# One attention-and-FFN decode kernel: its first group moved into the loop, TensorE's program walked in two outer trips, and w_down dealt unevenly over the partitions

## The chip, the cores and the metric

The kernel runs on one core of a Trainium2 chip. The metric is the device time of one execution in microseconds. The kernel before takes 292.81 us, the median of three runs (292.75 to 292.83).

## The reference

One decode step of a transformer block for two sequences (B = 2, one query each, D = 640): layer norm, attention of 32 heads of width 192 over the last 2048 positions of a cache, a residual, layer norm again, a gated FFN (F = 1536), a residual. All in bf16.

```python
q = (layernorm(x) @ wq)                       # [2, 32 heads, 192]
k = k_cache[:, :, 8192 - 2048:, :]            # [2, 32, 2048, 192]
v = v_cache[:, :, 8192 - 2048:, :]
p = softmax((q . k) * 192 ** -0.5)
h = x + (p . v).reshape(2, 1, 6144) @ wo
n = layernorm(h)
out = h + (gelu(n @ w_gate) * (n @ w_up)) @ w_down
```

Nearly all bytes are read once: 50 MB of keys, 50 MB of values, 7.9 MB each of wq and wo, and 5.9 MB of FFN weights.

## The kernel before, in words

**Groups.** The 2 x 32 heads are cut into 16 groups g of four heads of one sequence. A group's keys are one load of 24,576 bytes on each of 128 partitions, its values another. `transposes(g, half)` turns the keys on TensorE (48 transposes of 128 x 128 f32 words, each a pair of bf16) into two PSUM pairs, and VectorE (L588) and ScalarE (L584) copy them to SBUF. `scores(g)` multiplies them with the masked q (`rq`, made on POOL by `q_masked`), `softmax(g)` finds the maximum (L651, L653) and exponentiates (L655), `e_columns(g)` turns the probabilities (L664), `pv(g)` multiplies by the values (L680). After every fourth group `z_rows`, `o_rows`, `o_columns` and `oproj` make one quarter J of the heads' output and its product with wo.

**Order of the work.** It is written out by hand. `_Prog` records every operation with what it reads and writes, works out which semaphore value each must wait for, and prints each engine's program. TensorE's and VectorE's groups 1 to 15 stand in a loop of four trips (`emit_loop`), in segments named a0 to d2; four groups make a trip. In a loop a wait's value is linear in the trip: S x trip + a. Segments that only some trips need stand under an `If`: "oc" and "op" (o_columns and oproj of the quarter before), and d0 to d2, which the last trip leaves out. Group 0, with q's product (`q_rows`, L598: 80 matmuls; `q_stationary`, L616: 12), stands ahead of the loop, and group 15's rest and the FFN behind it.

**Loads.** All large loads are issued by SP in one order into a ring of six slots in SBUF (`load`, `pump`, L363): K0, wq, K1, V0, K2, V1 and so on, wo's quarters between them, then w_gate, w_up (two pieces) and w_down (four pieces). A load is issued when the pieces that lay in its place have been read. ScalarE issues x and the first fifth of w_gate.

**FFN.** `ffn_in` multiplies the normalized h with w_gate, later with w_up: for each of five chunks of 128 rows, four matmuls of 384 columns on four groups of 32 rows of the array. The 1536 results lie in four row groups r; `ffn_columns` (L831) turns them with three f32 transposes of 98 rows into columns of 128 partitions, twelve columns per sequence. VectorE and ScalarE make gelu of gate and the product with up (`uT`). w_down has 12 rows on each partition, in four pieces of 6, 3, 2 and 1 rows (`WDC`); each row takes four matmuls of 160 columns into `m1` (L871: 48 in all). VectorE copies the result (L877), and SP stores it (L878).

Of the kernel before, what the change touches and what calls it, by code (L numbers as in the profile page):

```python
# [27 lines left out]
LOOPED = ("pe", "dve")  # L28
RARE = ("oc", "op")

# [24 lines left out]
class _Prog:  # L55
# [63 lines left out]
    def resolve(self, strides):  # L119
# [110 lines left out]
TPG = 64  # L230
WDC = ((0, 6), (6, 9), (9, 11), (11, 12))
WUC = ((0, 4), (4, 5))
# [3 lines left out]
WQ_AT = 3 * SLOT + SLOT // 2  # L236
WO_AT = (K_AT[3], K_AT[3], K_AT[2], 0)
WD_AT = (K_AT[2] + 15360, 15360, 19200, 19200 + 2560)


def bass_sequential_preLN__sliding_block_cached__geglu_ffn__decode_kernel(
# [12 lines left out]
    with ExitStack() as ctx:  # L254
# [75 lines left out]
        urow = osb  # L330
        gsb = sb("gsb", [128, NF * B], F32)
        ga = sb("ga", [128, 4, NF * B], F32)
        uT = sb("uT", [128, NF, 18], BF16)

# [7 lines left out]
        P = _Prog()  # L342


# [51 lines left out]
        def load_ffn():  # L396
            load(("wg", 1), K_AT[1], 2 * (NC5 - 1) * F, B_w_gate.rearrange("(p c) f -> p c f", c=NC5)[:, 1:NC5, :],
                 lambda v: v.rearrange("p (c f) -> p c f", f=F), "wg1")
            for i, (c0, c1) in enumerate(WUC):
                load(("wu", i), K_AT[3] + 2 * c0 * F, 2 * (c1 - c0) * F, B_w_up.rearrange("(p c) f -> p c f", c=NC5)[:, c0:c1, :],  # L400
                     lambda v: v.rearrange("p (c f) -> p c f", f=F), f"wu{i}")
            wd = B_w_down.rearrange("(q p s) n -> q p s n", p=128, s=6)
            for i, (f0, f1) in enumerate(WDC):
                q = f0 // 6
                load(("wd", i), WD_AT[i], 2 * (f1 - f0) * D, wd[q][:, f0 - 6 * q:f1 - 6 * q, :],
                     lambda v: v.rearrange("p (s n) -> p s n", n=D), f"wd{i}")


        def dve(fn, R=(), W=(), X=(), cls=1):
            return P.op("dve", fn, R, W, X, cls=cls)  # L410

        def act(fn, R=(), W=(), X=()):
            return P.op("act", fn, R, W, X)

# [40 lines left out]

        dve(lambda e: e.memset(eps_t[:, :], EPS), W=["eps"])
        dve(lambda e: e.memset(onesd[:, :], 1.0 / D), W=["onesd"])
# [39 lines left out]

        pe(_x_T, R=["xrow", "identb"], X=["m2"])
        dve(lambda e: e.tensor_copy(xT[:, :, :].rearrange("p c b -> p (c b)"), m2[:, 0:10]), W=["xT"], X=["m2"])
# [91 lines left out]
        def q_rows():  # L591
            wq, wtoks = where["wq"]

            def fn(e):
                for c in range(NC5):
                    for J in range(4):
                        for r in range(4):
                            ins = e.matmul(tps[0][32 * r:32 * (r + 1), 0:384], lhsT=xnT[:, c, 32 * J:32 * (J + 1)],  # L598
                                           rhs=wq[:, c, 1536 * J + 384 * r:1536 * J + 384 * (r + 1)],
                                           start=(c == 0 and J == 0), stop=(c == NC5 - 1 and J == 3), tile_position=(0, 32 * r))  # L600
                return ins

            pe(fn, R=["xnT"] + wtoks, X=[("t", 0)], cls=1)
            done("wq")
            act(lambda e: e.activation(
                out=qrow[:, :, :, :],
                in_=tps[0][:, 0:384].rearrange("p (h d) -> p h d", h=2).unsqueeze(2).to_broadcast([128, 2, 2, DH]),
                func=ACT.Copy, scale=SCALE), W=["qrow"], X=[("t", 0)])

# [49 lines left out]
        def e_columns(g):  # L659

            def fn(e):
                for u in range(4):
                    o = m2[:, 0:256].rearrange("p (ch u x) -> p ch u x", ch=4, u=4)[:, :, u, :]
                    ins = e.matmul(o, lhsT=eexp[:, 128 * u:128 * (u + 1)], rhs=sel64[:, :], start=True, stop=True)  # L664
                return ins

            pe(fn, R=["eexp", "sel64"], X=["m2"])
            o = 8 * (g % 4)
            dve(tt(ering[:, g % 4, :, o:o + 8].rearrange("p (a h) x -> p a h x", h=2),
                   m2[:, 0:256].rearrange("p (a h x) -> p a h x", h=2, x=8),  # L670
                   mask16[:, :].rearrange("p (h x) -> p h x", h=2).unsqueeze(1).to_broadcast([128, 16, 2, 8]), ALU.mult),
                R=["mask16"], W=[("er", g % 4)], X=["m2"], cls=0)

# [80 lines left out]

        transposes(0, 0)
        transposes(0, 1)
        q_rows()
        q_stationary()
        consts_late()
        scores(0)  # L760
        softmax(0)
        for J in range(4):
            for p in range(1, 5 if J < 3 else 4):
                g = 4 * J + p
                seg = "abcd"[p - 1]
# [14 lines left out]
                pv(g - 1)  # L780
                scores(g)
                if p == 4:
                    o_rows(J)
                softmax(g)
# [28 lines left out]
        def ffn_in(bank, xt, key, parts, loads):  # L813
            for c0, c1 in parts:
# [3 lines left out]
                def fn(e, c0=c0, c1=c1, wv=wv, l0=loads[i][0]):  # L818
                    for c in range(c0, c1):
                        for r in range(4):  # L820
                            cols = wv[:, c - l0, 768 * (r // 2):768 * (r // 2 + 1)].rearrange("p (x s) -> p x s", s=6)
                            ins = e.matmul(bank[32 * r:32 * r + 2, 0:384], lhsT=hnT[:, c, :], rhs=cols[:, :, 3 * (r % 2):3 * (r % 2) + 3],
                                           start=(c == 0), stop=(c == NC5 - 1), tile_position=(0, 32 * r))
                    return ins
# [3 lines left out]
        def ffn_columns(row, tok, bank, i):  # L828
            def fn(e):
                for j in range(3):  # L830
                    ins = e.transpose(bank[:, 128 * j:128 * j + 98], row[0:98, j:384:3], identf[0:98, 0:98])  # L831
                return ins

            pe(fn, R=[*tok, "identf"], X=[("t", i)])
            return bank[:, 0:384].rearrange("p (j r y) -> p r j y", j=3, y=32)[:, :, :, 0:2]

# [5 lines left out]

        def rjb(t):
            return t.rearrange("p (r j b) -> p r j b", r=4, j=3)

# [4 lines left out]
        pe(h_rows, R=["hrow", ("hsel", 0), ("hsel", 1)], X=["m1"])  # L850
        gT = ffn_columns(grow, ["sm"], tps[0], 0)
        dve(lambda e: e.tensor_copy(rjb(gsb[:, :]), gT), W=["gsb"], X=[("t", 0)])
        dve(tt(ga[:, 0, :], gsb[:, :], gsb[:, :], ALU.mult), R=["gsb"], W=["ga0"])
# [9 lines left out]
        vT = ffn_columns(urow, [("osb", 0), ("osb", 1)], tps[1], 1)  # L863
        dve(tt(uT[:, :, 0:17:16].rearrange("p (r j) b -> p r j b", r=4), vT, rjb(ga[:, 0, :]), ALU.mult), R=["ga0"], W=["uT"], X=[("t", 1)])
        for i, (f0, f1) in enumerate(WDC):
            wd, wtoks = where["wd", i]

            def fn(e, f0=f0, f1=f1, wd=wd):
                for f in range(f0, f1):
                    for r in range(4):  # L870
                        ins = e.matmul(m1[32 * r:32 * r + 17, 0:160], lhsT=uT[:, f, 0:17],  # L871
                                       rhs=wd[:, f - f0, 160 * r:160 * (r + 1)], start=False, stop=(f == NF - 1),
                                       tile_position=(0, 32 * r), skip_group_check=True)
# [7 lines left out]

        P.resolve({("dve", 0): 4 * 9, ("dve", 1): 8, ("act", 0): 4 * 3, ("pool", 0): 4})
        sems = {}
        for e, c in (("pe", 0), ("pe", 1), ("act", 0), ("dve", 0), ("dve", 1), ("pool", 0)):
            sems[e, c] = ctx.enter_context(nc.semaphore(f"s_{e}{c}"))
# [37 lines left out]
```

## Time and profile before

| What | Value |
|---|---|
| median of three runs | 292.81 us |
| the profiled execution | 292.58 us |
| its span, first to last instruction | 291.3 us |
| TensorE matmul / weight load busy | 198.6 us (68%) / 147.6 us (51%) |
| VectorE / ScalarE / POOL busy | 122.8 us (42%) / 76.9 us (26%) / 25.7 us (9%) |
| bytes read, mean rate over the span | 122.29 MB, 420 GB/s |
| instructions | 5093 |
| granted TensorE clock, mean | 0.871 of full |

Busy times of engines add up to more than the span, since the engines run beside each other. A wait on an engine that is not the last costs nothing. The DMA rows of the page are the mean over the core's 16 DMA engines. "q1" is the queue of the kernel's large transfers, "q10" that of ScalarE's, "q8" and "q14" those over which programs' code is loaded. A transfer raises its semaphore step by step as the DMA engines that share it finish, and the trace records each step; a waiting instruction goes on at the last.

### The profile page before, as it was taken

How to read it: one execution, taken by the hardware profiler on the slowest of the kernel's cores; microseconds unless marked ns; L12 is line 12 of the kernel's file. 1: busy time of each engine (PE TensorE's matmuls, PEld its weight loads, DVE VectorE, ACT ScalarE, POOL GpSimd, SP SyncE). 2: the span in 40 equal slices, each digit the busy share in tenths (PEclk: the TensorE clock that was granted, in tenths of full speed). 3: DMA queues.
4: the chain of work that ended last, by engine and by line, in shares of the span. 5: the costliest groups of instructions: out<-in, count | busy, mean ns of one | idle time of the engine just before them, and what ended most of it. 6: DMA issues, size and time to landing. Idle time of an engine off the chain costs nothing.

```text
span 291.3 us, 5093 instructions
## 1 busy us (share of the span) xinstructions
PE 198.6 (68%) x2141; PEld 147.6 (51%) x2141; DVE 122.8 (42%) x231; ACT 76.9 (26%) x72; POOL 25.7 (9%) x85
## 2 busy tenths in 40 slices
PE   0650868786668288768677478868478778496684
PEld 0640437566355175637374475645465746472341
DVE  4350025455435334635356244635247445253331
ACT  1050014333322122423222123523142333151001
POOL 8820073000000000000000000000000000000000
PEclk9997568999979869997989579999689799688957
DMA  8999999999999999999999999999999999999994
GB/s 324 432 440 422 428 432 432 428 429 429 428 419 440 432 432 432 429 432 432 432 416 448 432 432 430 432 412 429 432 432 425 422 432 432 429 432 434 420 411 181
DMA packets 6506, 122.44 MB, mean 420 GB/s; under 512 B 734, under 2 KB 864, under 8 KB 1504
## 3 DMA queue, kind: packets, MB, share of 16 engines
q1 hardware_dynamic: 6348, 121.90, 97.8%
q10 hardware_dynamic: 148, 0.40, 0.4%
q8 instruction: 7, 0.11, 0.2%
q14 instruction: 3, 0.02, 0.0%
HBM read 122.29 MB, written 0.00 MB: 420 GB/s over the span
## 4 chain that ended last, share of the span: by engine, by line
DMA 73%; PE 18%; DVE 3%; issue 2%; SPq 2%; ACT 1%; DVEq 0%
DMA ring<-in_A_k_cache_dram 54%; PE tpp L574 13%; DMA ring<-in_A_wq_dram 10%; DMA ring<-in_B_w_down_dram 9%; DVE ktr L588 3%; PE tpp L598 2%; SPq L363 2%; PE ops L680 1%; DVE ering L428 1%; ACT ktr L584 1%; PE m L731 1%; PE m L713 1%; PE m L871 0%; PE m L694 0%; DVE yrow L877 0%
## 5 line engine op out<-in xcount | busy, mean ns | idle before, releaser
L574 PE MATMUL tpp<-identf,ring 128*128 128x128 f32 x768 | 116.2, 314 | 39.3 <-DMA ring<-in_A_k_cache_dram 25.2
L574 PEld LDWEIGHTS tpp<-identf,ring 128*128 128x128 f32 x768 | 102.8, 163 | 47.5 <-DMA ring<-in_A_k_cache_dram 26.5
L588 DVE COPY ktr<-tpp 128x2048 bf16<-128x2048 bf16 x64 | 78.4, 1224 | 91.4 <-PE tpp L574 91.4
L584 ACT ACTIVATE ktr<-tpp 128x2048 bf16<-128x2048 bf16 x32 | 60.1, 1877 | 94.9 <-PE tpp L574 94.9
L655 ACT ACTIVATE eexp<-sm,nm 128x512 bf16<-128x512 f32 x16 | 11.6, 722 | 71.7 <-DVE nm L653 71.7
L635 PE MATMUL sps<-ktr,rq 128*16 128x512 bf16 x384 | 25.7, 402 | 1.1 <-POOL rq L428 1.1
L680 PE MATMUL ops<-ring,ering 128*32 128x384 bf16 x512 | 25.0, 339 | 0.0
L644 DVE CUSTOM_DVE_ANT_1 sm<-sps,mska 128x512 f32<-128x512 f32 x16 | 11.0, 686 | 27.0 <-issue 27.0
L428 POOL TENSOR_TENSOR rq<-qs,mask 128x96 bf16<-128x96 bf16 x16 | 5.5, 354 | 175.6 <-PE sps L635 154.1
L680 PEld LDWEIGHTS ops<-ring,ering 128*32 128x32 bf16 x512 | 12.7, 99 | 8.5 <-issue 2.8
L635 PEld LDWEIGHTS sps<-ktr,rq 128*16 128x16 bf16 x384 | 8.9, 89 | 14.4 <-issue 5.5
L651 PEld LDWEIGHTS m<-mrhs,pm 128*128 128x128 bf16 x16 | 1.5, 96 | 22.9 <-DVE mrhs L424 22.9
L651 PE MATMUL m<-mrhs,pm 128*128 128x16 bf16 x16 | 2.9, 184 | 14.8 <-DVE mrhs L424 14.8
L598 PE MATMUL tpp<-ring,xnT 128*32 128x384 bf16 x80 | 6.1, 499 | 9.4 <-DMA ring<-in_A_wq_dram 9.4
L598 PEld LDWEIGHTS tpp<-ring,xnT 128*32 128x32 bf16 x80 | 3.4, 143 | 11.9 <-issue 9.6
L621 DVE CAST qs<-ops 128x384 bf16<-128x384 f32 x1 | 0.6, 558 | 15.8 <-PE ops L616 15.8
L428 DVE TENSOR_TENSOR ering<-m,mask 128x256 bf16<-128x256 f32 x16 | 6.6, 415 | 1.3 <-PE m L664 1.3
L713 PE MATMUL m<-selb,orow 128*128 128x2 bf16 x48 | 3.5, 200 | 5.2 <-DVE ering L428 4.5
L713 PEld LDWEIGHTS m<-selb,orow 128*128 128x128 bf16 x48 | 3.2, 159 | 6.0 <-DVE ering L428 4.9
L664 PE MATMUL m<-sel,eexp 128*128 128x64 bf16 x64 | 4.8, 200 | 1.2 <-ACT eexp L655 1.2
L494 PE MATMUL m<-identb,xrow 2*128 2x2 bf16 x5 | 0.3, 173 | 7.4 <-DMA xrow<-in_A_x_dram 7.4
L428 DVE TENSOR_TENSOR orow<-m,wm 128x1536 bf16<-128x1536 f32 x3 | 5.3, 1751 | 0.0
(127 smaller groups left out, 93.6 us busy)
## 6 DMA issues: line engine op xcount, KB each, us to landing
ring<-in_A_k_cache_dram SPq DMA_DIRECT2D x16, 3072.0 KB, 29.5
ring<-in_A_v_cache_dram SPq DMA_DIRECT2D x16, 3072.0 KB, 25.4
ring<-in_A_wq_dram SPq DMA_DIRECT2D x1, 7680.0 KB, 28.1
ring<-in_A_wo_dram SPq DMA_DIRECT2D x4, 1920.0 KB, 21.6
ring<-in_B_w_gate_dram SPq DMA_DIRECT2D x1, 1536.0 KB, 31.4
ring<-in_B_w_up_dram SPq DMA_DIRECT2D x1, 1536.0 KB, 21.9
ring<-in_B_w_down_dram SPq DMA_DIRECT2D x1, 960.0 KB, 24.3
ring<-in_B_w_down_dram SPq DMA_DIRECT2D x1, 480.0 KB, 25.0
```

The costliest lines, as they stand in the source:

```text
L363: P.op("sp", lambda e, v=v, src=src: e.dma_start(v, src), W=toks + [("sem", sem)], dma=sem)
L428: return lambda e: e.tensor_tensor(out=out, in0=a, in1=b, op=op)
L574: ins = e.transpose(tpp[bi][:, 512 * j + 128 * u:512 * j + 128 * (u + 1)], kv[:, off:off + 128], identf[:, :])
L584: act(lambda e, dst=dst, bv=bv: e.activation(out=dst, in_=bv, func=ACT.Copy), W=[("kt", half, k)], X=both)
L588: dve(lambda e, dst=dst, bv=bv: e.tensor_copy(dst, bv.rearrange("p (a x) -> p a x", a=2)), W=[("kt", half, k)], X=both, cls=0)
L598: ins = e.matmul(tps[0][32 * r:32 * (r + 1), 0:384], lhsT=xnT[:, c, 32 * J:32 * (J + 1)], rhs=wq[:, c, 1536 * J + 384 * r:1536 * J + 384 * ...
L635: ins = e.matmul(sps[32 * ch:32 * ch + 16, :], lhsT=rq[:, g % 4, k, :], rhs=ktr[:, k // 2, 1024 * ch + k % 2:1024 * (ch + 1):2], start=(k ...
L644: dve(lambda e: e.tensor_tensor_reduce(out=sm[:, :].rearrange("p (u x) -> p u x", u=4), in0=sps[:, :].rearrange("p (u x) -> p u x", u=4), ...
L655: act(lambda e: e.activation(out=eexp[:, :], in_=sm[:, :], func=ACT.Exp, bias=nm[:, 0:1], scale=1.0, accum_out=zr[:, g % 4:g % 4 + 1]), R= ...
L664: ins = e.matmul(o, lhsT=eexp[:, 128 * u:128 * (u + 1)], rhs=sel64[:, :], start=True, stop=True)
L680: ins = e.matmul(ops_[32 * r:32 * (r + 1), 0:384], lhsT=ering[:, g % 4, t, :], rhs=vv[:, 384 * t:384 * (t + 1)], start=(g % 4 == 0 and t < 4),
L713: ins = e.matmul(m2[:, 2 * kk:2 * kk + 2], lhsT=orow[:, :, kk:DH:12], rhs=selb[:, :], start=True, stop=True)
```

## The change

Three edits.

1. **The first group goes into the loop.** The loop's trips now begin with segment d (group 4J), followed by a, b, c (4J + 1 to 4J + 3). What trip 0 has alone, q_rows and q_stationary, is segment "q" under an `If`; what it lacks (the turn and the product of the group before, z_rows, o_rows) is "y0", "y1", "y2" under `If`s. The constants of `consts_late` are recorded ahead of it all, so they come before the masked q on POOL. To keep the waits of trip 0 linear and positive, some counters begin at 16 (`BIAS`), some operations change to another counter (`cls`).
2. **An early jump to the end of TensorE's program.** TensorE's program is put into an outer loop of two trips, under `If(i > 0)`: trip 0 branches over the whole program to the end of the outer loop and back, trip 1 does the work.
3. **w_down is dealt differently.** The first 1408 rows lie 11 to a partition on 128 partitions (pieces of 5, 3, 2 and 1 rows); the last 128 lie four to a partition on partitions 0 to 31 alone, in one transfer ("wds") ahead of the four. The matmuls and turns follow: `ffn_in` has five matmuls per chunk (three of 384 columns, one of 256, one of 128), `ffn_columns` nine transposes (three of 66 rows, two and four of two rows), the column tiles 16 columns per sequence, and w_down 16 + 44 matmuls.

```diff
-RARE = ("oc", "op")
+BIAS = 16
+RARE = ("oc", "op", "q", "y0", "y1", "y2")
...
-            n = {}
+            n = {c: BIAS for c in (1,) if e in LOOPED}
...
-            ins.then_inc(sems[o.key()], 1)
+            ins.then_inc(sems[o.key()], 1 + BIAS if o.cls == 1 and o.idx == 1 and o.eng in LOOPED else 1)
...
-WDC = ((0, 6), (6, 9), (9, 11), (11, 12))
+WDC = ((0, 5), (5, 8), (8, 10), (10, 11))
+NS = 11
+WDS_AT = K_AT[1] + 12288
...
-            wd = B_w_down.rearrange("(q p s) n -> q p s n", p=128, s=6)
+            load("wds", WDS_AT, 8 * D, B_w_down[128 * NS:F, :].rearrange("(c a u) n -> a c (u n)", a=8, u=4), lambda v: v[0:32, :], "wds")
+            wd = B_w_down[0:128 * NS, :].rearrange("(p s) n -> p s n", s=NS)
...
-        transposes(0, 0)
-        transposes(0, 1)
-        q_rows()
-        q_stationary()
         consts_late()
-        scores(0)
-        softmax(0)
+        looped.append(True)
         for J in range(4):
-            for p in range(1, 5 if J < 3 else 4):
+            for p in range(4):
                 g = 4 * J + p
-                seg = "abcd"[p - 1]
+                seg = "dabc"[p]
                 P.loop_seg(seg + "0", J)
                 transposes(g, 0)
-                e_columns(g - 1)
-                if p == 4:
-                    z_rows(J)
+                if p > 0:
+                    e_columns(g - 1)
+                elif J > 0:
+                    P.loop_seg("y0", J)
+                    e_columns(g - 1)
+                    z_rows(J - 1)
...
+                if p == 0 and J == 0:
+                    P.loop_seg("q", J)
+                    q_rows()
+                    q_stationary()
+                if p == 0 and J > 0:
+                    P.loop_seg("y1", J)
+                    pv(g - 1)
...
-                        for r in range(4):
-                            cols = wv[:, c - l0, 768 * (r // 2):768 * (r // 2 + 1)].rearrange("p (x s) -> p x s", s=6)
-                            ins = e.matmul(bank[32 * r:32 * r + 2, 0:384], lhsT=hnT[:, c, :], rhs=cols[:, :, 3 * (r % 2):3 * (r % 2) + 3],
-                                           start=(c == 0), stop=(c == NC5 - 1), tile_position=(0, 32 * r))
+                        cols = wv[:, c - l0, 0:128 * NS].rearrange("p (x s) -> p x s", s=NS)
+                        for r in range(3):
+                            e.matmul(bank[32 * r:32 * r + 2, 0:384], lhsT=hnT[:, c, :], rhs=cols[:, :, 3 * r:3 * r + 3],
+                                     start=(c == 0), stop=(c == NC5 - 1), tile_position=(0, 32 * r))
+                        e.matmul(bank[96:98, 0:256], lhsT=hnT[:, c, :], rhs=cols[:, :, 9:11], start=(c == 0), stop=(c == NC5 - 1),
+                                 tile_position=(0, 96), skip_group_check=True)
+                        ins = e.matmul(bank[96:98, 256:384], lhsT=hnT[:, c, :], start=False,
+                                       rhs=wv[:, c - l0, 128 * NS:F].rearrange("p (c a u) -> p a c u", c=4, a=8),
+                                       stop=(c == NC5 - 1), tile_position=(0, 96), skip_group_check=True)
...
-                    ins = e.transpose(bank[:, 128 * j:128 * j + 98], row[0:98, j:384:3], identf[0:98, 0:98])
+                    e.transpose(bank[:, 128 * j:128 * j + 66], row[0:66, j:384:3], identf[0:66, 0:66])
+                for j in range(2):
+                    e.transpose(bank[:, 128 * j + 96:128 * j + 98], row[96:98, j:256:2], identf[96:98, 96:98])
+                for u in range(4):
+                    ins = e.transpose(bank[0:32, 384 + 32 * u:386 + 32 * u], row[96:98, 256 + u:384:4], identf[96:98, 96:98])
...
+        def wds_rows(e):
+            for u in range(4):
+                for r in range(4):
+                    ins = e.matmul(m1[32 * r:32 * r + 17, 0:160], lhsT=uT[0:32, 12 + u, 0:17], rhs=wds[:, D * u + 160 * r:D * u + 160 * (r + 1)],
+                                   start=False, stop=False, tile_position=(0, 32 * r), skip_group_check=True)
+            return ins
...
-        order = ["a0", (0, None, ["oc"]), "a1", (0, 3, ["op"]), "a2", "b0", "b1", "b2", "c0", "c1", "c2", (None, 3, ["d0", "d1", "d2"])]
+        order = ["d0", (0, None, ["y0"]), "d1", (None, 1, ["q"]), (0, None, ["y1"]), "d2", (0, None, ["y2"]), "d3",
+                 "a0", (0, None, ["oc"]), "a1", (0, 3, ["op"]), "a2", "a3",
+                 "b0", "b1", "b2", "b3", "c0", "c1", "c2", "c3"]
         P.emit_loop("dve", nc.vector, sems, 4, order)
-        P.emit_loop("pe", nc.tensor, sems, 4, order)
+        with nc.tensor.Fori(0, 2) as i:
+            with nc.tensor.If(i > 0):
+                P.emit_loop("pe", nc.tensor, sems, 4, order)
```

More of the change, by code (lines that the diff above doesn't have):

```diff
@@ L401, in load_ffn, with act @@
                      lambda v: v.rearrange("p (c f) -> p c f", f=F), f"wu{i}")
-            wd = B_w_down.rearrange("(q p s) n -> q p s n", p=128, s=6)
+            load("wds", WDS_AT, 8 * D, B_w_down[128 * NS:F, :].rearrange("(c a u) n -> a c (u n)", a=8, u=4), lambda v: v[0:32, :], "wds")
+            wd = B_w_down[0:128 * NS, :].rearrange("(p s) n -> p s n", s=NS)
             for i, (f0, f1) in enumerate(WDC):
-                q = f0 // 6
-                load(("wd", i), WD_AT[i], 2 * (f1 - f0) * D, wd[q][:, f0 - 6 * q:f1 - 6 * q, :],
+                load(("wd", i), WD_AT[i], 2 * (f1 - f0) * D, wd[:, f0:f1, :],
                      lambda v: v.rearrange("p (s n) -> p s n", n=D), f"wd{i}")
         def dve(fn, R=(), W=(), X=(), cls=1):
-            return P.op("dve", fn, R, W, X, cls=cls)
-        def act(fn, R=(), W=(), X=()):
-            return P.op("act", fn, R, W, X)
+            return P.op("dve", fn, R, W, X, cls=cls if looped else 0)
+        def act(fn, R=(), W=(), X=(), cls=0):
+            return P.op("act", fn, R, W, X, cls=cls)
         def pe(fn, R=(), W=(), X=(), cls=0):
@@ L607, in q_rows @@
                 in_=tps[0][:, 0:384].rearrange("p (h d) -> p h d", h=2).unsqueeze(2).to_broadcast([128, 2, 2, DH]),
-                func=ACT.Copy, scale=SCALE), W=["qrow"], X=[("t", 0)])
+                func=ACT.Copy, scale=SCALE), W=["qrow"], X=[("t", 0)], cls=1)
         def q_stationary():
@@ L778, in bass_sequential_preLN__sliding_block_cached__geglu_ffn__decode_kernel @@
                     oproj(J - 1)
+                if p == 0 and J == 0:
[5 more added lines that the diff above has]
+                    pv(g - 1)
                 P.loop_seg(seg + "2", J)
-                pv(g - 1)
+                if p > 0:
+                    pv(g - 1)
                 scores(g)
-                if p == 4:
-                    o_rows(J)
+                if p == 0 and J > 0:
+                    P.loop_seg("y2", J)
+                    o_rows(J - 1)
+                P.loop_seg(seg + "3", J)
                 softmax(g)
@@ L870, in fn @@
                     for r in range(4):
-                        ins = e.matmul(m1[32 * r:32 * r + 17, 0:160], lhsT=uT[:, f, 0:17],
-                                       rhs=wd[:, f - f0, 160 * r:160 * (r + 1)], start=False, stop=(f == NF - 1),
+                        ins = e.matmul(m1[32 * r:32 * r + 17, 0:160], lhsT=uT[:, 4 * (f % 3) + f // 3, 0:17],
+                                       rhs=wd[:, f - f0, 160 * r:160 * (r + 1)], start=False, stop=(f == NS - 1),
                                        tile_position=(0, 32 * r), skip_group_check=True)
@@ L879, in bass_sequential_preLN__sliding_block_cached__geglu_ffn__decode_kernel @@
              dma="dout")
-        P.resolve({("dve", 0): 4 * 9, ("dve", 1): 8, ("act", 0): 4 * 3, ("pool", 0): 4})
+        P.resolve({("dve", 0): 4 * 9 - 1, ("dve", 1): 9, ("act", 1): 0, ("act", 0): 4 * 3, ("pool", 0): 4})
         sems = {}
-        for e, c in (("pe", 0), ("pe", 1), ("act", 0), ("dve", 0), ("dve", 1), ("pool", 0)):
+        for e, c in (("pe", 0), ("pe", 1), ("act", 0), ("act", 1), ("dve", 0), ("dve", 1), ("pool", 0)):
             sems[e, c] = ctx.enter_context(nc.semaphore(f"s_{e}{c}"))
```

27 lines of the change are left out of this document (15 added, 12 removed).

## The prediction

> **What bounds the kernel now.** I read the page's chain of work first, then its DMA rows, then the chain and the engines' timeline at the end.
>
> ```profile
> DMA 73%; PE 18%; DVE 3%; issue 2%; SPq 2%; ACT 1%; DVEq 0%
> ...
> DMA  8999999999999999999999999999999999999994
> ...
> q1 hardware_dynamic: 6348, 121.90, 97.8%
> ```
>
> The chain is transfers, and the DMA row stands at 9 from the second slice to the last but one. PE's 18% of the chain are steps that release a ring slot for a transfer which then waits its turn: a K load takes 29.5 us from issue to landing (page, part 6), and its own bytes take 7.3 us (V0's landing at 43.6 against K1's at 36.3). So TensorE may run some 15 us late inside the loop before a queue runs dry. What counts is when the last byte lands and what follows it. The chain from 255 us on:
>
> ```profile
> 262.97 25.38 DMA ring<-in_B_w_down_dram
> 288.39 0.75 PE m L871 x11
> 289.17 0.32 DVE yrow L877
> ```
>
> And the same stretch in the DMA view (window 255 to 291, 40 slices of 0.9 us):
>
> ```profile
> DMA  9998899999999899897989999999899999953000
> ```
>
> Before the last bytes there are slices at 9, 5 and 3: some DMA engines have finished while others still work. The trace's records of the semaphore steps show it: a transfer over 128 partitions lands in sixteen steps, one per DMA engine. The last w_down piece lands in steps at 286.89 to 287.02 (six), 287.23, 287.47, 287.57, 287.88, 288.38, and 288.61 to 288.76 (five). The last five set the end: 1.75 us behind the first six. wq's steps lie within 0.60 us (28.98 to 29.58). Where the delay comes from, by the DMA view of 30 to 100, 100 to 270 and 270 to 291 us:
>
> ```profile
> q8 instruction: 5, 0.08, 0.5%
> ```
>
> ```profile
> q14 instruction: 1, 0.01, 0.0%
> ```
>
> ```profile
> q8 instruction: 2, 0.03, 0.6%
> ```
>
> The first window has five code loads (16 KB each, at 33.4, 54.4, 64.3, 76.2, 92.7 us in the packet records), the second none (one 8 KB packet of q14), the third two (275.1, 287.4). Each takes about 1.0 us on one DMA engine. The records put packets back to back on an engine, so I can follow one: after the load at 64.35 its next data packet starts at 65.96, 1.61 us later than it would have. In the K landing after the first load one step is 1.75 us behind, at last five are: five loads, five engines, once each. The load at 275.1 accounts for the step at 288.38; that at 287.4 falls on an engine that was done.
>
> **The change, part by part.** The sums are against the profiled execution, 292.58 us (span 291.3 and 1.3 around it), 0.23 under the median of 292.81; 0.23 is added at the end.
>
> First group in the loop. TensorE's written code loses group 0's matmuls (48 transposes, 24 score products, one for the maximum; q's 80 and 12 only move), some 146 instructions of weight load and matmul, and gains branches and register waits; the order of work in time stays. It costs a few branches per trip (0.04 to 0.05 us each by the chain's DVEq rows) under the 15 us of cover: 0. The small constants are made before q on POOL's queue and no longer behind the masked q, so POOL is free sooner: also 0, as the first scores wait for wq's landing at 29.58. TensorE passes as many code pages in its first trip, or one fewer: four or five loads, each on an engine of its own. The largest delay stays at 1.75: 0.
>
> Early jump. The first trip of a new outer loop jumps over everything to the end, so the last code page or two load at 1 to 4 us. TensorE's first work, the transpose of x at 7.4, waits for x's landing at 7.26; if the jump costs two loads of 2 us it is still in time: 0 at the start, and if that cover is gone, K0's transposes start at 11.2 and q's product waits until 29.6. The step at 288.38 should join the rest, but it was not the last: 0.
>
> w_down, DMA side. The bytes stay 1.97 MB. Before, each engine carries 8 partitions x 12 rows x 1280 B = 122,880 B. Now 8 x 11 x 1280 = 112,640 B each, and 128 rows, 163,840 B, go in one more transfer whose outer extents are 8 (source) and 32. In the trace x (outer extent 2) lands in two steps and the output (4) in four, besides one at issue, so I count eight engines, 20,480 B each. Eight engines end with 133,120 B, eight with 112,640: 10,240 B up or down. An engine moves 24,576 B in 0.908 us, so 0.38 us later or earlier. If the five delayed engines are all among the relieved eight, the end comes 0.38 earlier (288.76 to 288.38; the loaded eight then end by 287.88 + 0.38 = 288.26). If one of the five is among the loaded eight, it comes 0.38 later. No row names an engine. What I can do is follow x's two packets (4.16 and 5.96 us): back to back as above, their engines are not those of the five loads, as far as engines a few ns apart can be told. [...] One issue more on SP is 0.43 us (median of the w_down issues) with 24 to 25 us to landing ahead of it: 0, and 0.43 without that lead.
>
> [...]
>
> The FFN's compute. Timeline of before:
>
> ```profile
> 277.85 1.30 PE L748 MATMUL m<-hsel,hrow 98*64 98x2 f32 x20
> ...
> 282.44 0.77 PE L831 MATMUL tpp<-identf,sm 98*128 98x98 f32 x3 [0.20 <-DVE sm L424]
> ...
> 283.13 1.67 PE L822 MATMUL ops<-ring,hnT 128*2 128x384 bf16 x20
> ...
> 285.49 0.59 PE L831 MATMUL tpp<-identf,osb 98*128 98x98 f32 x3 [0.69 <-ACT osb L861]
> 286.11 0.22 DVE L428 TENSOR_TENSOR uT<-tpp,ga 128x24 bf16<-128x24 f32 x1 [1.01 <-PE tpp L831]
> ...
> 286.51 0.59 PE L871 MATMUL m<-ring,uT 128*17 128x160 bf16 x24 [0.44 <-DMA ring<-in_B_w_down_dram]
> ```
>
> Each half's three transposes become nine. The three start 0.12 to 0.23 us apart. The six new ones move two columns; the nearest rows are the 65 ns of L748 (1.30 / 20) and those starts. Bounds: nothing (hidden) to 6 x 0.23 = 1.4 for gate (granted clock 0.54 in 277 to 284) and 6 x 0.12 = 0.7 for up (0.93 behind it). I take two wide ones at a start and four at 65 ns, less 0.1 for narrower old ones: 0.4 and 0.3. Gate's land on up, because TensorE goes straight on at 283.13 with w_up that landed at 283.07. Up's five matmuls instead of four per chunk stream the same 384 columns on each row group: 0, bound 0.1 x 5. VectorE on 32 columns, not 24: under 0.05. So uT is ready at 286.33 + 0.7 = 287.05 (bounds 286.33 to 288.95). Then 60 matmuls, not 48; the 24 of the first piece start 0.016 us apart at full clock, 0.032 at half. All but the last four: 287.05 + 56 x 0.016 = 287.95 at full, 288.84 at half clock; before, the last four start at 288.80. The clock went to half at 287.85, which gives 288.04, behind cover of the last landing at 288.38. So between -0.38 and +0.04; I take -0.3. What follows the last landing (four matmuls, the copy 0.32, the output) stays 2.5 us.
>
> Sum: 292.58 - 0.3 + 0.23 = **292.5**.
>
> **The rivals.** A, the above: the five are in the relieved eight, compute stays covered: 292.5.
> B, one of the five is in the loaded eight: 292.81 + 0.38 = 293.2. [...]
> C, slower, compute takes the transfers' place: the FFN's added transposes and w_down matmuls end last. It decides from uT later than 287.5 at full or 286.6 at half clock. At the far bound, 288.95 + 56 x 0.032 = 290.74 against 288.80, +1.9; midway between my value and that +1.0: 293.8. For it: six more transposes in each half and a clock that halves here; against it: TensorE waits in before for three of four pieces.
> D, two code loads fall on one engine, or one on the engine that is already 0.99 behind for other reasons (287.88): the last step moves by up to 1.6, less 0.38: up to 294.4 without relief. For it: the jump changes the order of loads; against it: seven loads on seven engines before.
> E, the early pages don't stay and the late loads come back, so the jump doesn't do what it says: the load at 275.1 leaves its engine at 288.38, and + 0.38 if that engine is loaded gives 288.76, the old end: 292.8. Against it: between 100 and 270 us TensorE goes through its loop again, some 950 matmul and weight-load instructions, without one load.
> [...]
> F, better balanced than I think, because a load at the very start delays nobody and another is saved: sixteen equal engines would end at the mean of the steps, 287.73, 1.0 earlier: 291.8.
>
> **How the numbers follow.** A 0.42, B 0.18, C 0.13, D 0.09, E 0.10, F 0.08. Within 0.2% of 292.81, which is about what a measurement of this kernel can tell from no change, is 292.22 to 293.40. Faster: F and 0.05 of A, 0.13. Slower: D, 0.09 of C and 0.05 of B, 0.23. Same: the rest, 0.64. The range 292.0 to 294.0 leaves out most of F and parts of C and D.
>
> **What would show it.** A: the last piece's sixteen steps spread 0.4 to 1.5 us less than 1.87 with no load behind 270 us; the one w_down transfer lands in eight steps besides the one at issue. B: five late steps at 2.1. C: the chain's last w_down transfer no longer ends at its landing, but matmuls follow without a wait for DMA. D: one step alone over 3 us behind. Wrong altogether: gaps in the DMA row inside the loop, that is, a late TensorE that starves the queue, which I gave no chance of its own.

## The result and the profile after

The changed kernel takes **293.69 us** (median of 12 runs, 293.0 to 294.53) against 292.80 for the kernel before (12 runs, 292.53 to 292.93) beside it: a ratio of 1.0030, 95% interval 1.0022 to 1.0037. It is slower by 0.9 us. The forecast was 292.5, 0.3 below before, with "no change" as the likeliest outcome (0.64). The time lies in the range of 292.0 to 294.0, but it moved the other way. The profiled execution took 293.69 us itself, its span 292.4.

The page's chain summary, and its row of code loads (packets, MB, share of 16 engines):

```profile
q8 instruction: 9, 0.15, 0.2%
...
DMA 71%; PE 19%; DVE 4%; issue 2%; SPq 1%; ACT 1%; DVEq 0%
```

DMA has lost two points of the chain, PE and DVE gained one each. Where, the chain of waits from 248 us on shows (start, length, what):

```profile
248.20 28.25 DMA ring<-in_A_wo_dram
276.45 0.04 issue
276.49 1.80 PE m L734 x13
...
283.48 0.63 DVE sm L427
284.11 0.04 issue
284.16 0.56 PE tpp L847 x3
284.71 0.33 PE tpp L849 x2
285.04 0.13 PE tpp L851 x4
...
286.93 0.59 ACT osb L881
287.52 0.04 issue
287.57 0.57 PE tpp L847 x3
288.13 0.32 PE tpp L849 x2
288.46 0.15 PE tpp L851 x4
288.61 0.02 issue
288.63 0.26 DVE uT L431
288.88 0.04 issue
288.93 0.45 PE m L890 x16
289.38 0.90 PE m L901 x44
290.28 0.02 issue
290.30 0.32 DVE yrow L907
```

Before, the chain's last transfer was w_down, landing at 288.76. Now it is the last quarter of wo, landing at 276.45; behind it stand 14 us of computing without one wait for a transfer. The last w_down bytes land at 289.09, when the 60 w_down matmuls are already running. In the DMA view (window 255 to 291, 40 slices) the transfers thin out much as they did:

```profile
DMA  9999999989999999999999999999999999974000
```

So the end has passed from the transfers to TensorE, VectorE and ScalarE. The stretches by window (us, busy time of each engine with its count, then the granted clock, DMA share and GB/s), first of before:

```profile
270.00:276.00 6.00, 3.66 (x56) 2.12 (x52) 2.56 (x4) 0.00 (x0) 0.00 (x0) 0.93 0.97 412
276.00:278.00 2.00, 1.40 (x30) 0.91 (x22) 0.55 (x3) 0.00 (x0) 0.00 (x0) 0.90 1.06 442
...
284.00:288.00 4.00, 2.37 (x51) 1.13 (x43) 0.96 (x5) 0.80 (x2) 0.00 (x0) 0.93 0.82 322
288.00:290.50 2.50, 0.72 (x12) 0.22 (x12) 0.32 (x1) 0.00 (x0) 0.00 (x0) 0.50 0.03 11
```

and of the changed kernel:

```profile
270.00:276.00 6.00, 5.53 (x58) 2.82 (x50) 2.38 (x3) 0.00 (x0) 0.00 (x0) 0.50 0.99 418
276.00:278.00 2.00, 1.51 (x24) 0.63 (x24) 0.18 (x1) 0.00 (x0) 0.00 (x0) 0.50 1.00 424
...
284.00:288.00 4.00, 3.17 (x37) 2.07 (x37) 1.58 (x8) 0.81 (x2) 0.00 (x0) 1.00 0.87 344
288.00:290.50 2.50, 1.91 (x68) 1.42 (x66) 0.44 (x2) 0.00 (x0) 0.00 (x0) 1.00 0.03 12
```

The clock column (the granted share of full speed) differs in both directions: half at 270 to 278, where before had 0.9, and full behind 284, where before fell to half at 288. So one pair of profiles mixes two things, the change and the clock, and experiments must part them. Three theories were put to the test. **Theory 1:** the jump costs, by its code loads, which delay the engine that lands wo's last quarter (0.73 us later than before) and with it all that follows. **Theory 2:** only the longer FFN of edit 3 costs, and the jump does no harm. **Theory 3:** the uneven bytes cost by themselves.

### The profile page after: what moved, and what is told of

It reads as the page before. It is cut to its first block, busy times and chain, and to the rows that moved or that the text cites. A ratio compares the mean times of both kernels' runs of the same rounds, so it can differ in the third digit from the quotient of the medians.

```text
span 292.4 us, 5231 instructions
## 1 busy us (share of the span) xinstructions
PE 197.8 (68%) x2175; PEld 148.5 (51%) x2175; DVE 123.1 (42%) x231; ACT 76.9 (26%) x72; POOL 25.9 (9%) x85
## 4 chain that ended last, share of the span: by engine, by line
DMA 71%; PE 19%; DVE 4%; issue 2%; SPq 1%; ACT 1%; DVEq 0%
DMA ring<-in_A_k_cache_dram 51%; PE tpp L577 11%; DMA ring<-in_A_wq_dram 10%; DMA ring<-in_A_wo_dram 10%; DVE ktr L591 3%; PE tpp L601 2%; SPq L366 1%; PE m L734 1%; PE ops L683 1%; DVE ering L431 1%; ACT ktr L587 1%; PE m L716 1%; PE sps L833 1%; PE m L751 0%; PE tpp L847 0%
## 5 line engine op out<-in xcount | busy, mean ns | idle before, releaser
L577 PE MATMUL tpp<-identf,ring 128*128 128x128 f32 x768 | 114.7, 311 | 43.5 <-DMA ring<-in_A_k_cache_dram 29.9
L638 PE MATMUL sps<-ktr,rq 128*16 128x512 bf16 x384 | 24.6, 389 | 1.4 <-POOL rq L431 1.4
L601 PE MATMUL tpp<-ring,xnT 128*32 128x384 bf16 x80 | 4.8, 414 | 9.1 <-DMA ring<-in_A_wq_dram 9.1
L601 PEld LDWEIGHTS tpp<-ring,xnT 128*32 128x32 bf16 x80 | 2.7, 120 | 11.0 <-issue 9.3
L734 PE MATMUL m<-ring,ot 128*2 128x320 bf16 x96 | 5.5, 381 | 0.5 <-DMA ring<-in_A_wo_dram 0.5
```

Of the source, the lines that this page charges most:

```text
L577: ins = e.transpose(tpp[bi][:, 512 * j + 128 * u:512 * j + 128 * (u + 1)], kv[:, off:off + 128], identf[:, :])
L638: ins = e.matmul(sps[32 * ch:32 * ch + 16, :], lhsT=rq[:, g % 4, k, :], rhs=ktr[:, k // 2, 1024 * ch + k % 2:1024 * (ch + 1):2], start=(k ...
L734: ins = e.matmul(m1[32 * r:32 * r + 2, 192:512], lhsT=ot[:, kk, :], rhs=wo[:, kk - k0, 320 * h:320 * (h + 1)], start=(kk == 1 or J < 2 and ...
```

## The experiments

All ran beside the kernel before, five rounds each; the times are medians, the ratios to before with 95% intervals.

**Without the jump** (loop and w_down edits stay).

```diff
-        with nc.tensor.Fori(0, 2) as i:
-            with nc.tensor.If(i > 0):
-                P.emit_loop("pe", nc.tensor, sems, 4, order)
+        P.emit_loop("pe", nc.tensor, sems, 4, order)
```

> The changed kernel without the early jump (first group in the loop and the uneven w_down stay). Theory 1 (the jump's code load falls on a DMA engine that is already late with ScalarE's w_gate piece, leaves it 2.6 us behind for the rest of the run, and so delays the last wo quarter by 0.7 us and everything computed from it): no code load before 30 us, no semaphore step more than 1.9 us behind the first, wo's last quarter lands at 275.7 instead of 276.5, time 293.0 (0.7 less than the changed kernel's 293.7). Theory 2 (the longer FFN alone makes it slower; the jump is harmless): 293.6 to 293.8, unchanged.

Measured: 293.94 us (293.17 to 294.27), 1.0041 (1.0029 to 1.0053). In this kernel's profile wo's last quarter does land earlier, at 275.59, and the last w_down matmuls still wait for no transfer. The jump is not the cost: theory 1 falls.

**Without the new w_down** (loop and jump stay; `WDC`, `ffn_in`, `ffn_columns` and the w_down loads as before).

```diff
-WDC = ((0, 5), (5, 8), (8, 10), (10, 11))
+WDC = ((0, 6), (6, 9), (9, 11), (11, 12))
```

> The first group in the loop and the early jump, with w_down and the FFN as before. Theory 1: one engine 2.6 us behind, nothing relieves it, so the last w_down piece lands at about 289.5 instead of 288.8: 293.5. Theory 2: the FFN is as before, so 292.8.

Measured: 292.66 us, 0.9998 (0.9989 to 1.0007).

**The new w_down alone** (edit 3 on the kernel before) and **the loop alone** (edit 1).

> The kernel before with the uneven w_down and its longer FFN alone. Both theories have the last bytes land 0.38 earlier (288.4) if the late engines are in the relieved half. Theory 1: the FFN's added 0.7 us still fits under the transfers, at least when the clock is full near the end: 292.4 to 292.7. Theory 2: the FFN ends last without any jump: 293.3 to 293.7, and the chain ends in matmuls that wait for no DMA.

> The kernel before with its first group moved into the loop alone. Both theories: the transfers are not touched, one code load fewer in the first trip, five late engines become four, the last step where it was: 292.7 to 292.9. A rival for either: the loop's branches and register waits make TensorE late and starve the queue: gaps in the DMA row and over 293.2.

Measured: w_down alone 293.57 us (293.26 to 294.55), 1.0032 (1.0020 to 1.0045); the loop alone 292.71, 0.9997 (0.9988 to 1.0006). The whole cost lies in edit 3; the loop and the jump cost nothing that can be measured.

Two of these kernels have nearly the same clock at the end, 0.50 to 0.52 from 278 us on, so their profiles can be set side by side: the loop alone and loop with w_down (the kernel without the jump). They differ by edit 3 alone. Their timelines (start, length, engine, line, operation, and in brackets the idle time before it and what ended that), first the loop alone:

```profile
275.74 0.98 PE L732 MATMUL m<-ring,ot 128*2 128x320 bf16 x24 [1.01 <-DMA ring<-in_A_wo_dram]
...
282.23 0.76 PE L840 MATMUL tpp<-identf,sm 98*128 98x98 f32 x3 [0.20 <-DVE sm L425]
...
283.14 1.77 PE L831 MATMUL ops<-ring,hnT 128*2 128x384 bf16 x20
...
285.60 0.76 PE L840 MATMUL tpp<-identf,osb 98*128 98x98 f32 x3 [0.69 <-ACT osb L870]
286.40 0.22 DVE L429 TENSOR_TENSOR uT<-tpp,ga 128x24 bf16<-128x24 f32 x1 [1.51 <-PE tpp L840]
...
288.41 0.70 PE L880 MATMUL m<-ring,uT 128*17 128x160 bf16 x12 [0.17 <-DMA ring<-in_B_w_down_dram]
```

then loop with w_down:

```profile
275.63 0.99 PE L734 MATMUL m<-ring,ot 128*2 128x320 bf16 x24 [2.12 <-DMA ring<-in_A_wo_dram]
...
286.17 0.61 PE L847 MATMUL tpp<-identf,osb 66*128 66x66 f32 x3 [0.67 <-ACT osb L881]
...
286.71 0.40 PE L849 MATMUL tpp<-identf,osb 2*128 2x2 f32 x2
...
286.97 0.27 PE L851 MATMUL tpp<-identf,osb 2*32 2x2 f32 x4
287.27 0.24 DVE L431 TENSOR_TENSOR uT<-tpp,ga 128x32 bf16<-128x32 f32 x1 [1.69 <-PE tpp L851]
287.57 0.71 PE L890 MATMUL m<-ring,uT 32*17 32x160 bf16 x16 [0.34 <-DVE uT L431]
288.21 1.65 PE L901 MATMUL m<-ring,uT 128*17 128x160 bf16 x44
```

`uT` starts 0.87 us later (287.27 against 286.40), and the last w_down matmuls no longer wait for their bytes. A table of the chain's terms, each from the first start to the last end in the trace, in us:

| | before | loop alone | loop + w_down | after | long FFN (below) |
|---|---|---|---|---|---|
| wo's last quarter lands at | 275.72 | 275.69 | 275.59 | 276.45 | 275.94 |
| last product with wo | 0.99 | 0.98 | 0.99 | 1.77 | 1.77 |
| gate's matmuls | 2.30 | 2.29 | 2.50 | 2.49 | 2.30 |
| gate's turns | 0.76 | 0.76 | 1.07 | 1.01 | 1.22 |
| up's matmuls | 1.67 | 1.77 | 1.97 | 1.80 | 1.77 |
| up's turns | 0.59 | 0.76 | 1.06 | 1.02 | 1.22 |
| uT ends at | 286.33 | 286.62 | 287.52 | 288.87 | 288.65 |
| last w_down matmul starts | 288.81 | 288.81 | 289.52 | 290.02 | 290.55 |
| last w_down bytes land | 288.76 | 288.75 | 289.07 | 289.09 | 288.95 |

In the two left columns the last matmul starts 0.05 to 0.06 us behind the last landing, in the others 0.45 to 1.6 us behind it. In the profile of the changed kernel uT ends 2.54 us later than before, but that is not all edit 3: 0.63 is the later start of the last product with wo and 0.78 its half clock, and the remaining 1.1 lies in what follows that product.

**The bytes without the FFN's work.** w_down's first row alone as a transfer meant for eight engines, on the kernel before:

```diff
-WDC = ((0, 6), (6, 9), (9, 11), (11, 12))
+WDC = ((0, 1), (1, 6), (6, 9), (9, 11), (11, 12))
...
+                if i == 0:
+                    load(("wd", 0), WD_AT[0], 2 * D, src.rearrange("(a b) s n -> a b (s n)", a=8), lambda v: v, "wd0")
+                    continue
```

> The kernel before, but w_down's first row of every partition comes as a transfer of its own whose outer extents are 8 and 16, so that (by the steps of wds) the same eight DMA engines that wds loads carry 10,240 B more and the other eight as much less; the FFN is that of before. Theory 2 (only the longer FFN costs, the uneven bytes themselves help by 0.3 to 0.4 us): 292.3 to 292.5, the last piece's last steps at 288.3 to 288.4 unless a code load falls on a loaded engine late. Theory 3 (the uneven bytes cost by themselves, for one of the late engines is among the loaded): 293.1 to 293.3.

Measured: 292.75 us, 1.0003 (0.9994 to 1.0012). This is inconclusive: the transfer landed in sixteen steps, not eight, so no bytes moved from engine to engine; that such a transfer shares the eight engines of wds was the author's estimate. It shows only that one more issue costs nothing that can be measured.

**The FFN's work without the uneven bytes**, wds dealt over sixteen engines:

```diff
-            load("wds", WDS_AT, 8 * D, B_w_down[128 * NS:F, :].rearrange("(c a u) n -> a c (u n)", a=8, u=4), ...
+            load("wds", WDS_AT, 8 * D, B_w_down[128 * NS:F, :].rearrange("(p u) n -> p (u n)", u=4), ...
```

> The kernel before with edit 3, but wds is dealt evenly over sixteen engines (32 partitions, one outer extent of 32), so bytes are even and the FFN is as long as in after. Theory 2: the compute chain still ends last whatever the bytes do, 293.4 to 293.7, yrow without a wait for DMA. Theory 3: 292.8, as the uneven bytes are gone.

Measured: 294.25 us, 1.0050 (1.0036 to 1.0063), above both expectations. The last bytes land at 290.61, 1.85 us later than before, so here the transfers end last again. GB/s in 40 slices of 0.4 us from 276 to 292, first w_down alone (wds on eight engines), then the even deal:

```profile
GB/s 430 461 492 430 369 430 369 399 492 461 492 269 369 422 374 444 368 467 405 416 400 416 438 365 400 323 314 294 208 150 19 0 0 0 0 0 0 0 0 0
```

```profile
GB/s 369 430 461 430 461 369 461 338 461 430 461 415 376 353 415 314 214 204 236 330 379 200 304 166 160 365 390 413 374 394 380 234 186 160 102 13 0 0 0 0
```

From 282 to 286 us the mean rate is 251 GB/s against 412 with w_down alone: while sixteen engines load wds, w_up's and w_down's packets take longer as well (the median 6400-byte packet of that stretch 414 ns instead of 248). It changed two things at once and tells nothing of the FFN. A variant asked whether the adjoining reads do it:

```diff
-.rearrange("(p u) n -> p (u n)", u=4)
+.rearrange("(c a u) n -> a c (u n)", a=16, u=4)
```

> Edit 3 on the kernel before, wds on 32 partitions by sixteen engines as in the even deal, but each engine's two reads are 80 KB apart instead of adjoining. In the even deal every packet of 282 to 286 us took 1.5 to 1.8 times as long, whatever its queue entry. If sixteen engines writing to the same 32 partitions do that: again 294.2, packets of 6400 bytes at 380 ns or more. If the adjoining reads do it: 293.5, packets of 6400 bytes at 250 ns.

Measured: 293.95 us, 1.0039 (1.0027 to 1.0051); the median 6400-byte packet of 282 to 286 us took 353 ns, and the last bytes landed at 289.99. Between the two expectations: most of the slowing stays with reads 80 KB apart. The time itself says little here, since in its profile the last matmul starts at 290.54, 0.55 us behind the landing, about where w_down alone has it (290.51). Whether it comes from sixteen engines on 32 partitions was not parted from other causes and stays open.

**Leaving out the added work, piece by piece** (each on the kernel before with edit 3). Without the six two-row transposes of each half:

```diff
-                for j in range(2):
-                    e.transpose(bank[:, 128 * j + 96:128 * j + 98], row[96:98, j:256:2], identf[96:98, 96:98])
-                for u in range(4):
-                    ins = e.transpose(bank[0:32, 384 + 32 * u:386 + 32 * u], row[96:98, 256 + u:384:4], identf[96:98, 96:98])
```

> The kernel before with edit 3, but each half's six two-row transposes are left out (the columns of u from rows 9 and 10 and of the last 128 are whatever the PSUM bank held). The comparison of the loop alone with loop and w_down gives the turns 0.31 us per half at half clock. Theory 2: uT 0.5 to 0.6 us earlier than with them, 60 matmuls behind it still end about with the transfers: 292.7 to 293.0. If the turns are not what costs (theory 2 by the matmuls alone): no change, 293.5.

Without wds's 16 matmuls:

```diff
-        pe(wds_rows, R=["uT"] + wtoks, X=["m1"])
```

> The kernel before with edit 3, but the 16 matmuls with wds are left out (its 128 rows are missing from the output), the transfer and the nine transposes stay. At half clock 16 x 0.032 = 0.52 us less behind uT, at full clock 0.26. Theory 2: 293.0 to 293.3. If the matmuls are covered: no change, 293.5.

With four matmuls per chunk instead of five:

```diff
-                        e.matmul(bank[96:98, 0:256], lhsT=hnT[:, c, :], rhs=cols[:, :, 9:11], ...
-                        ins = e.matmul(bank[96:98, 256:384], ... rhs=wv[:, c - l0, 128 * NS:F].rearrange("p (c a u) -> p a c u", c=4, a=8), ...
+                        ins = e.matmul(bank[96:98, 0:384], lhsT=hnT[:, c, :], rhs=cols[:, :, 8:11], ...
```

> The kernel before with edit 3, but each chunk of gate and up takes four matmuls of 384 columns instead of five (row group 96 then holds rows 8 to 10, not the last 128 rows). Loop alone against loop and w_down gives the fifth matmul 0.20 us in gate and 0.20 in up, at half clock, of which gate's is partly covered by w_up's landing: 293.2 to 293.4. If the matmuls of five stream in the time of four, as the prediction had it: 293.5.

Measured: without the transposes 292.90 us, 1.0005 (0.9996 to 1.0014); without wds's matmuls 292.94, 1.0012 (1.0003 to 1.0021); with four matmuls 293.61, 1.0026 (1.0014 to 1.0039), not to be told from edit 3 by its median. Its trace shows 1.77 and 2.30 us for up and gate instead of 1.95 and 2.50, but wo's last quarter landed 0.36 us later than with w_down alone, and the product with wo ran at half clock. Taking out either of the first two pieces brings the time back to within 0.25 us of before: in both profiles the last w_down matmuls wait for their bytes again.

All three left out at once (the combined diff of the three above):

> The kernel before with edit 3's uneven bytes, and all the work that edit 3 adds to the FFN left out: the six two-row transposes of each half, the fifth matmul of each chunk, wds's 16 matmuls (so the columns of u from rows 9 and 10 and of the last 128 rows are not the right ones). The FFN is then no longer than before and the transfers end last. Relief is real (step A: the loaded eight end at 288.3, the others at 288.4): 292.3 to 292.45. Relief is spent, because one late code load now meets an engine that still has bytes to move (in four profiles with edit 3 one step lands 0.3 to 0.7 us behind the other fifteen): 292.7 to 292.9.

Measured: 292.65 us (292.33 to 292.92), 0.9997 (0.9988 to 1.0006). The end of its chain:

```profile
263.73 25.01 DMA ring<-in_B_w_down_dram
288.74 0.04 issue
288.79 0.34 PE m L886 x4
```

The transfers end last, and the uneven bytes neither cost nor bring anything measurable: theory 3 falls, and relief is spent. (The median lies between the two bands expected, 0.05 below that for spent relief.) The steps of the last piece show how: fourteen by 288.28, then 288.55 and 288.74.

**The added work alone**, bytes as before: six more transposes into unused columns, row group 96's matmul cut in two, 12 more w_down matmuls into unused columns:

```diff
+                for j in range(2):
+                    e.transpose(bank[:, 384 + 2 * j:386 + 2 * j], row[96:98, j:256:2], identf[96:98, 96:98])
+                for u in range(4):
+                    ins = e.transpose(bank[0:32, 392 + 2 * u:394 + 2 * u], row[96:98, 256 + u:384:4], identf[96:98, 96:98])
...
+                for f in range(3 if f0 == 0 else 0):
+                    for r in range(4):
+                        e.matmul(m1[32 * r:32 * r + 17, 352:512], lhsT=uT[:, f, 0:17], rhs=wd[:, f, 160 * r:160 * (r + 1)], ...
```

> The kernel before with its bytes dealt as before, and only work of edit 3's size added to the FFN: six two-row transposes into unused columns behind the three of each half, row group 96's 384 columns as two matmuls (258 and 126), and 12 more w_down matmuls into unused columns of m1 ahead of the first piece's. The output is that of before. Theory 2 (the longer FFN alone is the cost): 293.4 to 293.7, as with edit 3, with the runs in two groups by whether the clock halves ahead of the last product with wo. If the FFN's length is covered and something else of edit 3 costs: 292.7 to 292.9.

Measured: 294.27 us (294.0 to 294.38), 1.0048 (1.0034 to 1.0062), 0.6 above the upper end expected. Its chain, with the landing at 288.95 nowhere in it:

```profile
288.43 0.23 DVE uT L428
288.66 0.04 issue
288.71 0.58 PE m L878 x9
289.29 1.63 PE m L882 x38
290.91 0.02 issue
290.94 0.32 DVE yrow L888
```

With bytes and code loads of before, the work alone is enough. It is necessary (left out, the cost goes) and sufficient: theory 2 stands. That it came out above edit 3 goes with the clock in the one execution profiled, which was half from 266.1 us to the end, so the last product with wo took 1.77 us. Two groups of runs were expected and all five lie in the upper one; why is not shown.

## Why the prediction was wrong, step by step

**The step that failed is "The FFN's compute": "uT is ready at 286.33 + 0.7 = 287.05", with all but the last four of the matmuls done by 288.04, "behind cover of the last landing at 288.38".** Measured, uT ended at 287.52 (loop and w_down, half clock) to 288.87 (after, full clock), beyond the points that rival C had named, 286.6 at half and 287.5 at full clock. With loop and w_down the last four started at 289.51, 0.44 us behind a landing at 289.07. C came true: matmuls follow without a wait for DMA. It had 0.13 of the chances; that its 293.8 lies near the 293.69 measured is luck, as it was the middle between the forecast and its far bound, not a sum. The terms:

- *The transposes* were sized right: 0.4 and 0.3 forecast, 0.25 to 0.31 (gate) and 0.30 to 0.43 (up) measured. That gate's turns "land on up" was right too.
- *Five matmuls instead of four: "0, bound 0.1 x 5".* Measured 0.2 in gate and 0.2 in up. In the trace the last of the five starts 0.36 us apart from chunk to chunk, the four 0.32. It is not the count: cut into 258 and 126 columns (long FFN) up takes 1.77 as with four. It is the piece of 256 columns, read two of every eleven, which takes longer than the long FFN's 258 columns, read three of every six. The rows of loop and w_down and of the long FFN (busy us, mean ns of one):

```profile
L835 PE MATMUL ops<-ring,hnT 128*2 128x256 bf16 x5 | 1.9, 447 | 0.0
```

```profile
L823 PE MATMUL ops<-ring,hnT 128*2 128x258 bf16 x5 | 1.7, 393 | 0.0
```

The 128-column piece takes 288 to 290 ns in both orders in which its columns were read: in blocks (loop and w_down, sixteen apart) or one after the other (the even deal). With row group 96's 384 columns read three of every eleven in one matmul, up took 1.77 again.
- *The clock.* The prediction took over the pattern of its one profile: full from 270.8 to 277.6, half to 284.4, full again to 287.85. With loop and w_down it was half from 278 us on, so the first 56 of the 60 matmuls took 1.94 us (287.57 to 289.51) and not 0.99 (287.05 to 288.04). In that execution it is the largest of the missing terms. And in 8 of the 14 profiled executions the clock was half during the last product with wo, which then takes 1.77 us instead of 0.98. That is 0.79 us which the transfers' cover has to hide ahead of the FFN.

So the cover was the mis-sized number. In the loop alone, uT's end, the start of the products 0.06 later and 44 matmuls x 0.0325 us give 288.11 at half clock, 0.64 us ahead of the landing at 288.75; with the product with wo at half clock as well, nothing is left (288.90). The loop with the jump shows that case: last matmuls at 289.33 behind a landing at 289.13, in an execution of 293.14 us, the longest of its eleven. Edit 3 adds 0.9 to uT and 12 x 0.0325 = 0.39 in w_down, 1.3 in all, on 0.64 or on nothing: 0.65 or 1.3 later. By the table the last matmul starts 0.71 later with loop and w_down (product at full clock); w_down alone, with the product at half clock, has it at 290.51, 1.70 later. That is 0.4 more than 1.3: against loop and w_down, wo's last quarter landed 0.14 us later there, and the way from that landing to uT took 12.77 us, not 11.93. The runs of w_down alone fall in two groups, 293.26 to 293.61 and 294.29 to 294.55. That the clock makes the two groups is a reading of the profiled executions, not an experiment: no run here set the clock.

**w_down's DMA side.** Eight engines was right: wds lands in eight steps besides the one at issue (263.57). No run names the engines: that -0.38 and not +0.38 went into the sum was the author's estimate, and what the runs showed in its place are the steps. That the five late engines lie in the relieved half was right: in the kernel with the work left out, steps of 288.61 to 288.76 moved to 288.19 to 288.28, about as -0.38 says. But "The step at 288.38 should join the rest" was wrong. Take wds's eight steps there and subtract the 0.8 us that its bytes take (four packets of 201 ns): the last (284.40) belongs to the engine whose step for w_up was 283.61, the one with the late code load. It is loaded, so it ends at 288.38 + 0.38 = 288.76 (measured 288.74), which is rival E's price: the end stays where it was. So -0.38 was 0. In the changed kernel itself it was worse: the sixteen steps spread 2.39 us (286.70 to 289.09), where A wanted 0.4 to 1.5 less than 1.87. The loaded engines end by 288.82, and one step alone, of an engine that wds does not load, comes at 289.09, 0.33 later than before: rival D in part.

**Loop edit: 0** and **early jump: 0**: right as times (292.71 and 292.66). As a mechanism the jump does not do what it says. Code loads by windows 0 to 30, 30 to 100 and 270 to 293 us of the changed kernel:

```profile
q8 instruction: 2, 0.03, 0.4%
```

```profile
q8 instruction: 4, 0.07, 0.4%
```

```profile
q8 instruction: 3, 0.05, 0.8%
```

Two early loads (at 4.4 and 10.6 us, not 1 to 4; 0.96 and 0.98 us each, not 2) are added, and the late ones come back (270.3, 283.3, 290.8): E in that part. Between 100 and 270 us TensorE's loop of some 950 matmul and weight-load instructions runs without a load on q8, as in before, so against E that window settled nothing; why the late loads come back is not shown.

"0 at the start" did not hold. The record of the branch over the program lasts from 0.99 to 6.68 us, and the transpose of x starts at 7.56 instead of 7.40, though x had landed at 6.45. More than that, two of K0's sixteen steps land at 12.66 and 13.50, all others by 11.37 (before, all by 11.17): as many late steps as early loads. K0's transposes start at 13.54 and q's product at 31.78, not at the 11.2 and 29.6 that the prediction gave even for a lost cover. The loop hid this, as the time without the new w_down shows. But rival F's "a load at the very start delays nobody" fails by it: the latest step stays 2.6 us behind the first from K0's landing to the last K landing, and by that steady distance it is the same engine that brings wo's last quarter and w_down's last bytes late in the changed kernel's profile (276.45 and 289.09). Without the new w_down the profile shows the same with 2.3 us (276.09 and 289.13). Whether it costs a few tenths in every execution the times do not show.

**"What follows the last landing" at 2.5 us** failed with the cover: in after it is the span's end less 289.09, 3.3 us.

## What to carry to other kernels

When transfers and a compute chain end within a microsecond of each other, a gain on the one side is worth at most the margin of the other, so work out the margin before costing an edit, and at half as well as full granted clock: one profile shows one clock pattern (half during the last product with wo in 8 of 14 here). Here an edit that took 0.38 us from eight DMA engines put 1.3 us on a chain with 0 to 0.64 us to spare. Uneven shares pay only if the slowest unit of every kind is among the relieved (here one late engine was loaded, and with the added work left out the last landing moved from 288.76 to 288.74); look for the second-latest step too, which takes over.

No version here beats both kernels: with all of the added work left out the uneven bytes still gave 292.65 us against 292.75, within the interval of no change.

## What the runs showed that was not expected

- Taking six two-column transposes more costs as much at full clock as at half: up's turns grew by 0.43 us in after (0.59 to 1.02, full clock) and by 0.30 at half clock (0.76 to 1.06).
- While sixteen engines loaded 160 KB into 32 partitions, the other packets of those 4 us were slower too (median of 6400 bytes: 414 ns with adjoining reads, 353 with reads 80 KB apart) than with wds on eight engines (248).
- Up's matmuls, which read two or three of every eleven columns, gained little from the full clock: 1.80 us in after against 1.97 at half with loop and w_down, where the product with wo takes 0.99 against 1.77.
- A transfer with outer extents 8 and 16 over adjoining partitions landed in sixteen steps; one with extents 8 and 4, whose source blocks lie apart, in eight.
- The record of the branch over the whole program on TensorE lasts 5.69 us (0.99 to 6.68).
- With two code loads ahead of 11 us (4.4 and 10.6), two steps of K0's landing came 1.3 and 2.1 us behind the other fourteen, and at the last K landing one step was still 2.6 us behind the first.
